# A landmark-attention, FFN and routed-experts kernel: where its zeros are stored, and the order in which its first batch is emitted

## The chip, the cores and the metric

The kernel runs on one core of one Trainium2 chip. The metric is the device time of one execution in microseconds (us); three executions of the kernel before took 683.63, 684.98 and 687.62 us, so its median is 684.98 us. The profile was taken in a further execution that took 681.71 us. The engines are named as the profile names them: PE (TensorE, the matmuls), PEld (its weight loads), DVE (VectorE), ACT (ScalarE), POOL (GpSimd) and SP (SyncE, which here issues nearly all DMAs, one after the other; SPq is its DMA queue).

## What is computed

The reference chains three parts. The shapes are 4 batches, 8 heads, 576 tokens, head size 64, so 2304 tokens of 512 numbers.

```
q_lm, k_lm = means of q, k over 32 groups of 18 tokens
A, B, C = softmax(q k_lm'), softmax(q_lm k_lm'), softmax(q_lm k)
Z = B' / (norm1(B) * norminf(B) + 1e-6);  six times: Z = 2 Z - Z B Z
x = A Z C v                                  # -> 2304 x 512
x = relu(x w_in)**2 w_out                    # w_in 512x2048, w_out 2048x512
logits = x w_gate                            # 8 experts
each token goes to its best expert e (at most 576 tokens in one):
out[token] = prob(e) * (relu(x w1[e]) w2[e]) # w1 512x1024, w2 1024x512
```

The FFN weights w_in and w_out arrive as 64-bit floats, and the chip has to make 32-bit ones of their two words.

## The kernel before, in words

**Precision.** The matmuls of FFN and experts take operands in a short float format. Each operand is split into a high and a low part (h and l at the end of a name: `gh`, `gl`, `ah`, `al`, the pairs of `w` and `mw`), and three products are summed. Making these parts costs DVE and ACT work beside each PE group.

**Conversion of the weights.** `Convert` does one of 32 units (16 of w_in, 16 of w_out) in steps, each of which is a letter in the tables below: `a` takes the words of the high half (L200 on DVE, or L202 on ACT), `b` those of the low half (L207, L209), `d` shifts and merges integers on DVE (L214, L215), `j` joins the two on DVE (L219), `s` rounds a w_out unit to its high part (L224 on DVE, or L226 on ACT), and `l` makes its low part (L229). The letters `h`, `c`, `t` and `p` are the same steps on the other engine. A joined pair of w_in units is stored in DRAM again (`w_in<-wi`, L1196) and read back later, one block of columns at a time (`wi<-w_in`, L514).

**Stages.** Per batch of 576 tokens: attention (jobs named K, Q, LK, LQ, BS, BE, BN, FR, C, CE, CM, N, T, CV, Z, SP, A, AE, AN), which ends in the matrix `mt` and in the pair `ah`, `al`; a projection, which folds `mt` into w_in (L531 matmuls, ACT copy L187, DVE L533) and gives `mw`; and the FFN. The FFN runs in two halves of 288 tokens over 16 chunks of 128 hidden numbers. A chunk is an "up" (six matmuls L544, then relu `r` L547 on ACT, square `gg` on ACT L550 or POOL L552, high part `gh` L555 on ACT, low part `gl` L558 on DVE) and, two chunks later, a "down" (twelve matmuls L564 into four accumulators `acc`). Batch 0 switches between its halves after 6, 12, 8, 4 and 2 chunks; at a switch DVE takes the accumulators over (`x<-acc,x`, L947), and the next down waits for that.

**After a half** is done an epilogue writes the tokens with their gate to the token table `x2d` in DRAM (`x2d<-xr`, L1012), and routing scatters their numbers to a table per expert (`tab`, POOL, L881). The rows of `x2d` that belong to batch 3 and the whole output are filled with zeros on the way (`x2d<-z`, `out_dram<-z`). The experts then run over gathered tokens and scatter their results.

**Order.** Per engine, instructions run in the order in which the program emits them, as a scheduler arranges it. `FIRST` is the order of the attention jobs and conversion steps of batch 0 ahead of the FFN. `PLAN` has one entry for each place between the groups of the FFN at which `fill()` may emit something else: E, M, A and X take the next job of the epilogue, the projection, the attention and the experts, and the letters take a conversion step. `ORDER` is the order of the attention jobs of the other batches. SP's queue, DVE and ACT work strictly through their rows, so that an instruction that waits holds up those behind it.

**The zeros.** `prefill()` runs behind the first finished half of batch 0. It makes a tile `z` of zeros on chip and issues the three small stores (L582 to L585) and the zeros of the late `x2d` rows: 96 x 24 runs of 128 numbers, 1152 KB (L588), and a small rest (L589). `CLEAR` names three halves, (1, 0), (1, 1) and (2, 0), and behind each of them `clear()` emits two of the six output stores of 768 KB (L597). Their only input is `z`, and the scheduler put all six next to those of `prefill()`.

Of the kernel before, what the change touches and what calls it, by code (L numbers as in the profile page):

```python
# [40 lines left out]
RB0 = 3.2  # L41
RB = 2.6

ORDER = "K0 K1 K2 K3 LK Q0 Q1 Q2 Q3 A00 LQ A01 BS AE0 C00 BE C01 BN AN0 C10 CM0 C11 FR CE0 CM1 N0 T00 CE1 N1 T01 SP0 N2 CV0 N3 A10 T10 N4 A11 T11 AE1 N5 CV1 AN1 Z SP1".split()
PLAN = (
    ".MdlAsddja .ptbt . .aapbl . .Ap . .dtbsdaljtdAl .A . .daAbdpaljtbjAdb .ptjj .dp . .j .a . .bd .tbttaphAap  "
    ".jbAbtMpaAA .b .dj .adjt . . . . . .apA .dp . .btAjdAAsappbdMjta .b . . . .jdl . .b . .jMjptlA . . . .ad . .l  "
    ".b . .b .jbAdjAAja . .adaM .sAd . . . .jAjlb .l .Attp .j .aAA . .ta .t .apba .Ad .j .Ad . .bAsApbd . .adb .b  "
    ".Mb .bjp . .Mlt . . .ldld .jt .bj . . . .Abb .tasAbAtA .j .lA .dMhtdAjA .dtA .AMdlb .pa . . .jjp . . . . . .At  "
# [3 lines left out]
).split()  # L53
FIRST = (
    "b K0 CO Q0 K1 K2 K3 Q1 Q2 Q3 LK LQ BS a BE BN FR C00 C01 j N0 CM0 d CE0 l a N1 N2 C10 b C11 a N3 j CM1 N4 h  "
    "T00 CE1 d T01 a d CV0 T10 b d T11 A00 j CV1 N5 Z p a b p A01 j d AE0 b AN0 j t j t b t d j SP0 a l "
).split()
P = 96
F32 = mybir.dt.float32
F32R = mybir.dt.float32r  # L60
# [14 lines left out]
def tile_landmark_attention__ffn__routed_experts(ctx, tc, q, k, v, w_in, w_out, w_gate, e_w1, e_w2, out, cap):  # L75
    nc = tc.nc
    B, _, H, _ = q.shape
    _, _, S, D = v.shape
    NT, DM = out.shape
# [5 lines left out]
    R = S // P  # L85
# [9 lines left out]
    K2 = F2 // 128  # L95
# [14 lines left out]
    x2d = tc.dram_tile([NT + 1, DM + 1], F32, name="x2d")  # L110
# [384 lines left out]
    def attention(b):  # L495
        names = attn_stages(b)
        return [job(names, n) for n in ORDER]

# [3 lines left out]
    def job(names, n):  # L502
        c = COST.get(n, COST.get(n[:2], COST[n[0]]))
        return (free if n[:2] == "SP" else always, names[n], c)
# [66 lines left out]
            tc.declare_no_dep(op.ins, o.ins.name, reason="each scatter writes the rows of other tokens")  # L571
        scatters[key].append(op)

    zero = []

    def prefill():
        def f():
            z = xp.tile([128, 128], F32, name="z")
            n = xp.tile([128, E * TE // 128], I32, name="n")
            nc.vector.memset(z, 0.0)  # L580
            nc.vector.memset(n, NT)
            nc.sync.dma_start(out=tab.rearrange("(p c) o -> p (c o)", p=128), in_=n)  # L582

            nc.sync.dma_start(out=x2d[NT:NT + 1, 0:DM], in_=z[0:4, :])
            nc.sync.dma_start(out=x2d[NT:NT + 1, DM:DM + 1], in_=z[0:1, 0:1])  # L585
            late = x2d[NT - S:NT, :].rearrange("(p r) x -> p (r x)", r=R)
            n = R * DM // 128
            nc.sync.dma_start(out=late[:, 0:n * 128].rearrange("p (c x) -> p c x", x=128), in_=z[:P, :].unsqueeze(1).to_broadcast([P, n, 128]))  # L588
            nc.sync.dma_start(out=late[:, n * 128:], in_=z[:P, 0:R])  # L589
            zero.append(z)  # L590
        return [f]

    def clear(i, of):
        def f():
            rows = out.rearrange("(p r) (c x) -> p (r c) x", p=128, x=128)
            n = rows.shape[1] // of
            nc.sync.dma_start(out=rows[:, i * n:(i + 1) * n, :], in_=zero[0].unsqueeze(1).to_broadcast([128, n, 128]))  # L597
        return f

    CLEAR = [(1, 0), (1, 1), (2, 0)]  # L600
# [353 lines left out]
    def epilogue(b, hf, acc):  # L954
# [51 lines left out]
        def store():  # L1006
            xr = s["xr"]
            sm = xp.tile([P, RP], F32, tag="sm", name="sm", bufs=2)
            nc.vector.tensor_reduce(out=sm, in_=s["ex"], axis=AX.X, op=ALU.add)
            nc.vector.tensor_scalar_add(sm, sm, 1e-9)  # L1010
            nc.vector.reciprocal(out=xr[:, :, DM], in_=sm)
            nc.sync.dma_start(out=x2d[b * S:(b + 1) * S, :].rearrange("(p r a) c -> p a r c", p=P, a=2)[:, hf], in_=xr)  # L1012

        st = [rows(1), rows(2), store]
        head = {0: [logits, token_logits, gates, rows(0)], 1: [logits, rows(0), token_logits, gates], 2: [logits, rows(0), rows(1), token_logits, gates]}[EO]
# [2 lines left out]
        if hf == (LAST0 if b == 0 else 1):  # L1018
# [12 lines left out]
            n = len(st)  # L1031
# [12 lines left out]

    planq = deque(x[1:] for x in PLAN)
    tick, clock, gstep, slow = [None], [0], [0], [0]
# [37 lines left out]
    def ffn(seq, before, after):  # L1084

        pend, acc = deque(), None
        for t in range(len(seq) + 2):
# [215 lines left out]
    for i, n in enumerate(RUNS):  # L1303
        hf = i % 2
# [42 lines left out]
```

## Time and profile before

| | us |
|---|---|
| median of three runs | 684.98 |
| the profiled execution | 681.71 |
| its span in the trace | 679.7 |
| PE busy | 616.6 (91%) |
| DVE busy | 342.6 (50%) |
| ACT busy | 302.1 (44%) |
| POOL busy | 119.1 (18%) |

Busy time is a sum over the span, and a stage can be bound by an engine whose sum is small. A view by windows tells where each engine is full. Each row of a list of instructions has its start, its duration, the engine, the line and the tiles, and in brackets the idle time of that engine just before it with what ended it. The granted clock of PE is given as a share of its full speed (1.00 is 2.4 GHz, 0.50 is 1.2 GHz).

### The profile page before, as it was taken

What the parts mean: (1) busy time and instruction counts of PE and PEld (TensorE: products, weight loads), DVE (VectorE), ACT (ScalarE), POOL (GpSimd) and SP (SyncE); (2) the same over time, 40 slices, a digit from 0 to 9 for tenths busy, and PEclk for the clock granted to TensorE, in tenths of its full rate; (3) what the DMA queues carried; (4) which work ended last, traced back from release to release, by engine and by line L of the source; (5) the groups of instructions that cost most, each with busy time, mean ns of one, the idle gap of its engine ahead of it and who ended that gap; (6) DMA issues with size and microseconds to landing.
All of it is one profiled execution on the core that took longest, in us unless ns stands there. A gap on an engine that the chain in (4) does not pass through costs nothing. (4 is left out here: it accounts for less than half of the span.)

```text
span 679.7 us, 13567 instructions
## 1 busy us (share of the span) xinstructions
PE 616.6 (91%) x5322; PEld 523.6 (77%) x5322; DVE 342.6 (50%) x915; ACT 302.1 (44%) x710; POOL 119.1 (18%) x152
## 2 busy tenths in 40 slices
PE   3158779999798999999999999999999999999993
PEld 1035658988686878888889888889998889789792
DVE  8998998634642364532363533335543515416310
ACT  4863756554434453444354444245522524415420
POOL 0000000000012021222431212442315013104101
PEclk9999869999899999999999999999999999999997
DMA  9996442499136122331400022333307417306400
GB/s 317 378 401 182 163 124 70 158 212 278 63 103 100 56 70 71 107 123 65 80 20 21 17 94 94 66 104 99 93 9 230 154 34 256 100 16 208 159 10 35
DMA packets 44021, 83.91 MB, mean 123 GB/s; under 512 B 7494, under 2 KB 22090, under 8 KB 43178
## 3 DMA queue, kind: packets, MB, share of 16 engines
q1 hardware_dynamic: 40762, 75.18, 37.3%
q0 software_dynamic: 3184, 7.75, 3.4%
q8 instruction: 45, 0.74, 0.5%
q14 instruction: 30, 0.25, 0.1%
HBM read 64.52 MB, written 18.39 MB: 122 GB/s over the span
## 5 line engine op out<-in xcount | busy, mean ns | idle before, releaser
L564 PE MATMUL acc<-gh,w 128*128 128x288 f32 x1024 | 234.8, 303 | 7.0 <-DVE x L947 3.4
L564 PEld LDWEIGHTS acc<-gh,w 128*128 128x128 f32 x1024 | 173.3, 191 | 19.0 <-issue 7.5
L564 PE MATMUL acc<-gl,w 128*128 128x288 f32 x512 | 153.1, 303 | 0.0
L544 PE MATMUL hp<-ah,mw 128*128 128x288 f32 x512 | 131.7, 311 | 2.4 <-ACT mw L187 1.4
L558 DVE TENSOR_TENSOR gl<-gg,gh 128x288 fp32r<-128x288 f32 x128 | 60.5, 474 | 97.9 <-POOL gg L552 59.5
L544 PEld LDWEIGHTS hp<-ah,mw 128*128 128x128 f32 x512 | 91.7, 194 | 16.7 <-issue 10.6
L564 PEld LDWEIGHTS acc<-gl,w 128*128 128x128 f32 x512 | 97.2, 190 | 8.0 <-issue 4.7
L547 ACT ACTIVATE r<-hp 128x288 f32<-128x288 f32 x128 | 51.8, 409 | 99.5 <-PE hp L544 98.4
L552 POOL TENSOR_TENSOR gg<-r 128x288 f32<-128x288 f32 x80 | 54.9, 688 | 196.9 <-ACT r L547 184.2
L544 PE MATMUL hp<-al,mw 128*128 128x288 f32 x256 | 78.1, 306 | 0.0
L685 PE MATMUL acc<-w,ehh 128*128 128x512 f32 (+1 forms) x240 | 76.0, 397 | 0.0
L881 POOL DMA_INDIRECT tab<-toks,slot x24 | 22.6, 941 | 222.1 <-ACT gh L555 198.9
L555 ACT ACTIVATE gh<-r 128x288 fp32r<-128x288 f32 x128 | 56.1, 440 | 9.8 <-PE acc L564 5.5
L677 DVE SCALAR_TENSOR_TENSOR ehl<-hp,ehh 128x320 fp32r<-128x320 f32 (+1 forms) x48 | 21.9, 456 | 65.4 <-ACT ehh L676 65.4
L544 PEld LDWEIGHTS hp<-al,mw 128*128 128x128 f32 x256 | 50.0, 195 | 1.7 <-issue 1.5
L685 PEld LDWEIGHTS acc<-w,ehh 128*128 128x128 f32 (+1 forms) x240 | 41.6, 177 | 11.6
L685 PE MATMUL acc<-w,ehl 128*128 128x512 f32 (+1 forms) x120 | 47.3, 394 | 0.0
L533 DVE TENSOR_TENSOR mw<-ps,mw 128x256 fp32r<-128x256 f32 x64 | 25.4, 419 | 40.9 <-ACT mw L187 40.8
L187 ACT ACTIVATE mw<-ps 128x256 fp32r<-128x256 f32 x64 | 22.5, 383 | 49.4 <-PE ps L531 49.3
L676 ACT ACTIVATE ehh<-hp 128x320 fp32r<-128x320 f32 (+1 forms) x48 | 19.7, 411 | 43.9 <-PE hp L672 41.6
L531 PE MATMUL ps<-wi,mt 64*32 64x256 f32 x512 | 32.1, 407 | 5.1 <-DMA wi<-w_in 1.8
L689 ACT ACTIVATE y<-acc,gt 128x512 f32<-128x512 f32 (+1 forms) x15 | 10.3, 686 | 56.2 <-PE acc L685 41.3
(253 smaller groups left out, 947.9 us busy)
## 6 DMA issues: line engine op xcount, KB each, us to landing
raw<-in_moe_w_dram SPq DMA_DIRECT2D x32, 512.0 KB, 4.7
wi<-w_in SPq DMA_DIRECT2D x24, 512.0 KB, 3.4
w<-in_moe_w_in_dram SPq DMA_DIRECT2D x16, 512.0 KB, 8.8
w<-in_moe_w_out_dram SPq DMA_DIRECT2D x16, 512.0 KB, 11.9
x2d<-xr SPq DMA_DIRECT2D x8, 577.1 KB, 4.6
out_dram<-z SPq DMA_DIRECT2D x6, 768.0 KB, 10.7
w_in<-wi SPq DMA_DIRECT2D x8, 512.0 KB, 6.0
kT<-in_k_dram SPq DMA_DIRECT2D x3, 1152.0 KB, 9.0
```

Source lines behind the costliest of these rows:

```text
L187: nc.scalar.activation(out=o, in_=i, func=AF.Copy)
L531: nc.tensor.matmul(out=ps[s, :FC], lhsT=mt[rows, c, :], rhs=wi[rows, c, :], start=True, stop=True)
L533: nc.vector.tensor_tensor(out=ml[:, g, :], in0=ps[:, :FC], in1=f32(mh[:, g, :]), op=ALU.subtract)
L544: nc.tensor.matmul(out=hp[:, :HB], lhsT=st[:, g, fs], rhs=mv[:, g, :], start=n == 0, stop=n == 5)
L547: nc.scalar.activation(out=r, in_=hp[:, :HB], func=AF.Relu)
L552: nc.gpsimd.tensor_tensor(out=gg, in0=r, in1=r, op=ALU.mult)
L555: nc.scalar.activation(out=gh, in_=r, func=AF.Square)
L558: nc.vector.tensor_tensor(out=gl, in0=gg, in1=f32(gh), op=ALU.subtract)
L564: nc.tensor.matmul(out=acc[d][:, :HB], lhsT=w2[fc][:, st, ds], rhs=mv, start=first and i == 0, stop=last and i == 2)
L677: nc.vector.scalar_tensor_tensor(out=hl[:, f, :n], in0=hp[:, :n], scalar=0.0, in1=f32(hh[:, f, :n]), op0=ALU.max, op1=ALU.subtract)
L685: nc.tensor.matmul(out=acc[:n, :], lhsT=h[:, f, off:off + n], rhs=w2[f][:, w, :], start=f == 0 and a == 0, stop=f == K2 - 1 and a == 2)
L881: return lambda: scattered("tab", nc.gpsimd.indirect_dma_start(out=tab[:, :], out_offset=bass.IndirectOffsetOnAxis(ap=sl[:, r:r + 1], axis=0),
```

## The change

Two things. The first: the two zero stores of the late `x2d` rows leave `prefill()` and go to the first `clear()`, and everything in `clear()` is emitted behind the last stored token rows (`tc.issue_after(stored[-1])`); the store L1012 puts itself on that list. The second: new tables. In `ORDER` the job CM0 stands ahead of AN0. `FIRST` and `PLAN` are rewritten; the tables hold the same jobs, and over both of them two roundings of w_out units go from DVE to ACT and one `a` step from ACT to DVE.

```diff
-ORDER = "K0 K1 K2 K3 LK Q0 Q1 Q2 Q3 A00 LQ A01 BS AE0 C00 BE C01 BN AN0 C10 CM0 C11 FR ...
+ORDER = "K0 K1 K2 K3 LK Q0 Q1 Q2 Q3 A00 LQ A01 BS AE0 C00 BE C01 BN CM0 AN0 C10 C11 FR ...
-PLAN = (
-    ".MdlAsddja .ptbt . .aapbl . .Ap . .dtbsdaljtdAl .A . .daAbdpaljtbjAdb .ptjj .dp . .j .a . .bd .tbttaphAap  "
...
+PLAN = '.lMalAsdtd .bjs .p .aabl .A .AAapp . .taljAtdbA .jdAd .s .tdAbalpjtbAdb .pdtjj .djp . . .a .d .dat .bspha ...
-    "b K0 CO Q0 K1 K2 K3 Q1 Q2 Q3 LK LQ BS a BE BN FR C00 C01 j N0 CM0 d CE0 l a N1 N2 C10 b C11 a N3 j CM1 N4 h  "
-    "T00 CE1 d T01 a d CV0 T10 b d T11 A00 j CV1 N5 Z p a b p A01 j d AE0 b AN0 j t j t b t d j SP0 a l "
+FIRST = 'Q0 K0 CO b K2 K3 K1 Q3 Q2 LK Q1 LQ BS BE BN FR C00 j b C01 N0 d CM0 N1 l CE0 a N2 C10 b C11 N3 N4 a CM1 h a d j T00 CE1 T01 d CV0 T10 T11 A00 j CV1 b N5 p d Z a b A01 b d j p AE0 b j t d t t j a AN0 SP0'.split()
 P = 96
...
-    zero = []
+    zero, stored = [], []
 
     def prefill():
         def f():
...
             nc.sync.dma_start(out=x2d[NT:NT + 1, 0:DM], in_=z[0:4, :])
             nc.sync.dma_start(out=x2d[NT:NT + 1, DM:DM + 1], in_=z[0:1, 0:1])
-            late = x2d[NT - S:NT, :].rearrange("(p r) x -> p (r x)", r=R)
-            n = R * DM // 128
-            nc.sync.dma_start(out=late[:, 0:n * 128].rearrange("p (c x) -> p c x", x=128), in_=z[:P, :].unsqueeze(1).to_broadcast([P, n, 128]))
-            nc.sync.dma_start(out=late[:, n * 128:], in_=z[:P, 0:R])
             zero.append(z)
         return [f]
 
     def clear(i, of):
+
         def f():
-            rows = out.rearrange("(p r) (c x) -> p (r c) x", p=128, x=128)
-            n = rows.shape[1] // of
-            nc.sync.dma_start(out=rows[:, i * n:(i + 1) * n, :], in_=zero[0].unsqueeze(1).to_broadcast([128, n, 128]))
+            z = zero[0]
+            with tc.issue_after(stored[-1]):
+                if i == 0:
+                    late = x2d[NT - S:NT, :].rearrange("(p r) x -> p (r x)", r=R)
+                    n = R * DM // 128
+                    nc.sync.dma_start(out=late[:, 0:n * 128].rearrange("p (c x) -> p c x", x=128), in_=z[:P, :].unsqueeze(1).to_broadcast([P, n, 128]))
+                    nc.sync.dma_start(out=late[:, n * 128:], in_=z[:P, 0:R])
+                rows = out.rearrange("(p r) (c x) -> p (r c) x", p=128, x=128)
+                n = rows.shape[1] // of
+                nc.sync.dma_start(out=rows[:, i * n:(i + 1) * n, :], in_=z.unsqueeze(1).to_broadcast([128, n, 128]))
         return f
...
-            nc.sync.dma_start(out=x2d[b * S:(b + 1) * S, :].rearrange("(p r a) c -> p a r c", p=P, a=2)[:, hf], in_=xr)
+            stored.append(nc.sync.dma_start(out=x2d[b * S:(b + 1) * S, :].rearrange("(p r a) c -> p a r c", p=P, a=2)[:, hf], in_=xr).ins)
```

What the tables do to the engines shows in the order of their instructions. Line numbers of the kernel after are smaller by 11 ahead of the zeros and by 7 behind them; a number behind a name tells tiles of one name apart.

**SP, from the first small zeros on.** `vt`, `qT` and `ld` are loads of batch 2, the last row of the first piece is a load of a block of w_in. Before:

```order
L582 DMA tab<-n 128x40
L585 DMA x2d<-z 1x1
L588 DMA x2d<-z 96x24x128
L589 DMA x2d<-z 96x6
L597 DMA out_dram<-z 128x12x128 x6
L514 DMA wi<-w_in_69 128x1024
L277 DMA vt<-in_v_dram 96x4x384
L238 DMA qT<-in_q_dram 128x2304
L273 DMA ld<-in_v_dram 96x2x384 x2
```

After, from the store of the first half of batch 1 on (here `vt`, `qT` and `ld` are those of batch 3):

```order
L227 DMA kT<-in_k_dram 128x2304
L1005 DMA x2d<-xr 288x1x513
L586 DMA x2d<-z 96x24x128
L587 DMA x2d<-z 96x6
L590 DMA out_dram<-z 128x12x128 x2
L266 DMA vt<-in_v_dram 96x4x384
L227 DMA qT<-in_q_dram 128x2304
L262 DMA ld<-in_v_dram 96x2x384 x2
L503 DMA wi<-w_in_69 128x1024 x6
L1005 DMA x2d<-xr 288x1x513
L590 DMA out_dram<-z 128x12x128 x2
```

The large zeros went from ahead of the loads of batch 2 to behind the stores of batch 1 and 2, and the first group of them now stands ahead of the loads of batch 3; the last two output stores follow the next store of token rows.

**DVE, at the switch of halves in batch 0** at which the four sums `x<-acc,x` free the accumulators. `partq` is made from `qT` of batch 2. Before:

```order
L251 TENSOR_REDUCE partq<-qT 128x64 x4
L462 TENSOR_TENSOR T<-T,asm 128x576
L558 TENSOR_TENSOR gl<-gg,gh 128x288
L947 TENSOR_TENSOR x_1630<-acc_2030,x_1630 128x288
L947 TENSOR_TENSOR x_1630<-acc_2031,x_1630 128x288
L469 STREAM_TRANSPOSE at<-T 128x576
L947 TENSOR_TENSOR x_1630<-acc_2032,x_1630 128x288
```

After:

```order
L240 TENSOR_REDUCE partq<-qT 128x64 x4
L450 RECIPROCAL asm<-asm 128x18
L940 TENSOR_TENSOR x_1606<-acc_2025,x_1606 128x288
L940 TENSOR_TENSOR x_1606<-acc_2026,x_1606 128x288
L547 TENSOR_TENSOR gl<-gg,gh 128x288
L940 TENSOR_TENSOR x_1606<-acc_2027,x_1606 128x288
L940 TENSOR_TENSOR x_1606<-acc_2028,x_1606 128x288
L451 TENSOR_TENSOR T<-T,asm 128x576
```

The sums moved ahead of the attention's division of `T` and of the transpose into `at`; `partq` stays ahead of them.

**ACT, between the first chunks of the FFN.** `w_953` and `w_981` before, `w_956` and `w_982` after, are w_out units that have just been loaded. Before:

```order
L187 ACTIVATE mw<-ps 128x256 x2
L202 ACTIVATE w_953<-w_953 128x512
L209 ACTIVATE w_953<-w_953 128x512
L547 ACTIVATE r<-hp 128x288
L202 ACTIVATE w_981<-w_981 128x512
L550 ACTIVATE gg<-r 128x288
L555 ACTIVATE gh<-r 128x288
L209 ACTIVATE w_981<-w_981 128x512
```

After:

```order
L539 ACTIVATE gg<-r 128x288
L544 ACTIVATE gh<-r 128x288
L176 ACTIVATE mw<-ps 128x256
L198 ACTIVATE w_956<-w_956 128x512
L439 ACTIVATE T<-T 128x576
L191 ACTIVATE w_982<-w_982 128x512
L198 ACTIVATE w_982<-w_982 128x512
```

Relu and square of the third chunk stood behind the first conversion of a new unit; now the chunks' steps stand ahead of it (four chunks are through by then), and the other half of that step, L200, went to DVE.

## Rows read from the trace of the kernel before

**Rows 1.** Windows: busy us (instructions) of each engine, granted clock, DMA share, GB/s.

```profile
51.00:68.00 17.00, 13.69 (x105) 9.05 (x104) 15.00 (x31) 6.75 (x17) 0.00 (x0) 1.00 0.62 183
68.00:85.00 17.00, 13.37 (x102) 10.64 (x102) 15.84 (x34) 12.07 (x30) 0.00 (x0) 0.90 0.48 162
85.00:102.00 17.00, 12.99 (x90) 9.09 (x91) 16.52 (x38) 9.33 (x23) 0.00 (x0) 0.70 0.42 124
102.00:119.00 17.00, 17.00 (x143) 15.12 (x142) 15.22 (x38) 10.40 (x28) 0.00 (x0) 1.00 0.23 71
```

**Rows 2.** Timeline of PE: idle time ahead of matmuls of the ramp.

```profile
53.98 0.61 PE L544 MATMUL hp<-ah,mw 128*128 128x288 f32 x1 [1.36 <-ACT mw L187]
...
70.89 1.33 PE L564 MATMUL acc<-gh,w 128*128 128x288 f32 x4 [2.06 <-ACT gh L555]
...
87.09 0.69 PE L436 MATMUL ps<-qT,lmk 64*32 64x288 f32 x8 [2.33 <-DVE mw L533]
```

**Rows 3.** Timeline of ACT: waits for loaded units, and what stood behind one.

```profile
68.08 0.72 ACT L202 ACTIVATE w<-w 128x512 f32<-128x512 f32 x1 [7.05 <-DMA w<-in_moe_w_out_dram]
...
88.38 0.70 ACT L202 ACTIVATE w<-w 128x512 f32<-128x512 f32 x1 [3.44 <-DMA w<-in_moe_w_in_dram]
...
89.50 0.67 ACT L187 ACTIVATE ah<-at 128x576 fp32r<-128x576 f32 x1
```

**Rows 4.** Timeline of DVE: steps of the conversion.

```profile
57.62 0.65 DVE L219 CUSTOM_DVE_ANT_0 ct<-w,ct 128x1024 uint16<-128x1024 uint16 x1
58.31 0.43 DVE L224 CAST w<-ct 128x512 fp32r<-128x512 f32 x1
58.77 0.69 DVE L229 TENSOR_TENSOR w<-ct,w 128x512 fp32r<-128x512 f32 x1
59.49 0.43 DVE L214 TENSOR_SCALAR ct<-w 128x512 int32<-128x512 int32 x1
...
60.23 0.68 DVE L215 SCALAR_TENSOR_TENSOR ct<-w,ct 128x512 int32<-128x512 int32 x1
```

**Rows 5.** Timelines of SP's queue and DVE: the queries of batch 1, asked for and used.

```profile
65.38 0.33 SPq L238 DMA_DIRECT2D qT<-in_q_dram  x1
...
75.09 2.74 DVE L251 TENSOR_REDUCE partq<-qT 128x64 f32<-128x576 f32 x4
```

**Rows 6.** Timeline of SP's queue: the output zeros, and the queries of batch 2.

```profile
136.12 18.68 SPq L597 DMA_DIRECT2D out_dram<-z  x6
...
159.75 0.35 SPq L238 DMA_DIRECT2D qT<-in_q_dram  x1
```

**Rows 7.** Timelines of DVE and PE at the switch of halves in batch 0.

```profile
169.53 2.73 DVE L251 TENSOR_REDUCE partq<-qT 128x64 f32<-128x576 f32 x4 [5.02 <-DMA qT<-in_q_dram]
...
173.22 0.81 DVE L947 TENSOR_TENSOR x<-acc,x 128x288 f32<-128x288 f32 x2
...
173.72 0.61 PE L564 MATMUL acc<-gh,w 128*128 128x288 f32 x1 [3.42 <-DVE x L947]
```

**Rows 8.** Windows (columns as in rows 1) during the zeros, and around that switch.

```profile
140.00:145.00 5.00, 5.00 (x65) 4.54 (x50) 2.00 (x5) 2.69 (x8) 0.00 (x0) 1.00 1.22 137
...
150.00:155.00 5.00, 5.00 (x55) 4.28 (x55) 1.33 (x4) 2.02 (x6) 0.00 (x0) 1.00 1.11 326
...
170.00:175.00 5.00, 1.58 (x21) 1.28 (x6) 5.00 (x11) 0.91 (x3) 0.00 (x0) 0.83 0.31 106
175.00:180.00 5.00, 5.00 (x37) 4.26 (x35) 3.76 (x10) 0.77 (x2) 0.00 (x0) 0.83 0.00 0
```

**Rows 9.** The page's DMA issues: KB each, median us from issue to landing.

```profile
out_dram<-z SPq DMA_DIRECT2D x6, 768.0 KB, 10.7
...
x2d<-z SPq DMA_DIRECT2D x1, 1152.0 KB, 14.5
```

**Rows 10.** Timelines of SP's queue and DVE in batch 1, where the zeros go.

```profile
258.95 0.56 SPq L1012 DMA_DIRECT2D x2d<-xr  x1
...
276.42 0.34 SPq L238 DMA_DIRECT2D qT<-in_q_dram  x1
...
282.27 2.75 DVE L251 TENSOR_REDUCE partq<-qT 128x64 f32<-128x576 f32 x4 [0.66 <-DMA qT<-in_q_dram]
```

**Rows 11.** Timeline of PE: a wait behind the scatters of batch 0.

```profile
215.21 0.62 PE L531 MATMUL ps<-wi,mt 64*32 64x256 f32 x4 [1.78 <-DMA wi<-w_in]
```

More of the change, by code (lines that the diff above doesn't have):

```diff
@@ L42 @@
 RB = 2.6
-ORDER = "K0 K1 K2 K3 LK Q0 Q1 Q2 Q3 A00 LQ A01 BS AE0 C00 BE C01 BN AN0 C10 CM0 C11 FR CE0 CM1 N0 T00 CE1 N1 T01 SP0 N2 CV0 N3 A10 T10 N4 A11 T11 AE1 N5 CV1 AN1 Z SP1".split()
-PLAN = (
-    ".MdlAsddja .ptbt . .aapbl . .Ap . .dtbsdaljtdAl .A . .daAbdpaljtbjAdb .ptjj .dp . .j .a . .bd .tbttaphAap  "
-    ".jbAbtMpaAA .b .dj .adjt . . . . . .apA .dp . .btAjdAAsappbdMjta .b . . . .jdl . .b . .jMjptlA . . . .ad . .l  "
-    ".b . .b .jbAdjAAja . .adaM .sAd . . . .jAjlb .l .Attp .j .aAA . .ta .t .apba .Ad .j .Ad . .bAsApbd . .adb .b  "
-    ".Mb .bjp . .Mlt . . .ldld .jt .bj . . . .Abb .tasAbAtA .j .lA .dMhtdAjA .dtA .AMdlb .pa . . .jjp . . . . . .At  "
[3 rows of a table removed]
-).split()
-FIRST = (
-    "b K0 CO Q0 K1 K2 K3 Q1 Q2 Q3 LK LQ BS a BE BN FR C00 C01 j N0 CM0 d CE0 l a N1 N2 C10 b C11 a N3 j CM1 N4 h  "
-    "T00 CE1 d T01 a d CV0 T10 b d T11 A00 j CV1 N5 Z p a b p A01 j d AE0 b AN0 j t j t b t d j SP0 a l "
-).split()
+ORDER = "K0 K1 K2 K3 LK Q0 Q1 Q2 Q3 A00 LQ A01 BS AE0 C00 BE C01 BN CM0 AN0 C10 C11 FR CE0 CM1 N0 T00 CE1 N1 T01 SP0 N2 CV0 N3 A10 T10 N4 A11 T11 AE1 N5 CV1 AN1 Z SP1".split()
+PLAN = '.lMalAsdtd .bjs .p .aabl .A .AAapp . .taljAtdbA .jdAd .s .tdAbalpjtbAdb .pdtjj .djp . . .a .d .dat .bspha .bMbpA .jAabd .d .ajt . .t . .jl . .AapA .d .bb .bjdtaatppbddMj .blt .A . . .jj .b . . .jptj . .A .p .d . .laj .bA .d .b .jAa .Aba .tAadaM . .p .A . .jAjb .td .A .Aj .AalA .ap .tp .tA .bMh .l .dbaj .Ad . .bsb . .dd .Apb .Mjb .bjp .Ma .ls . .A .d .tj .Mj .l . .l .bt .tsAAcAA .jtt .cl .dhhAj .A .AMdl .pA . .t .pt .db . . . . .Aj . .ddAA . .p . . . . . . .A .A .A .d . . .Mt . .tbA .A . .A . .h .Ad . .a . .Aa .A .A . . . . . . .M . .A . .j .l . . . . . . . . . .E .EElEA .E .E . .a . . . . . .EEE .EE . .E . . . .EEE .ME .E . . . . . . .EEs . . .lEMEE .bM .EEEA . . . . . . . . . . . . .j .sA'.split()
+FIRST = 'Q0 K0 CO b K2 K3 K1 Q3 Q2 LK Q1 LQ BS BE BN FR C00 j b C01 N0 d CM0 N1 l CE0 a N2 C10 b C11 N3 N4 a CM1 h a d j T00 CE1 T01 d CV0 T10 T11 A00 j CV1 b N5 p d Z a b A01 b d j p AE0 b j t d t t j a AN0 SP0'.split()
 P = 96
```

3 rows, old and new, of the table PLAN are left out of this document.

## The prediction

> **What bounds the kernel now.** I read the windows first, since 91% busy of PE hides where it is not. PE is full from about 100 us on, but in the three windows from 51 to 102 us it is busy 13.69 + 13.37 + 12.99 = 40.05 of 51 us [rows 1]: 10.95 us are idle, and in two of them the granted clock is under 1.00. There DVE is busy 47.36 of 51 us. So the ramp, where the weights are still being converted, is bound by DVE, with 3.64 us in which DVE too waits; at 102 to 119 us PE has taken over. Next I read the timeline of PE for what ends its gaps [rows 2]: copies of ACT (`mw`, `gh`) and DVE's `mw`. The waits of ACT tell why ACT is late though it is half idle: it stood 7.05 us at a freshly asked w_out unit and 3.44 us at a w_in unit [rows 3], with relu, `gh` and `ah` queued behind. Last, the only wide gap after the ramp is 3.42 us at 173.72 [rows 7]: PE waits for the sums that free its accumulators, these stand on DVE behind `partq`, and `partq` had waited 5.02 us for `qT`. The load was asked for at 159.75 and in use at 169.53, 9.78 us; that of the next batch took 276.42 to 282.27, 5.85 us [rows 6, 10]. What lies between is 1152 KB + 6 x 768 KB of zeros, whose last issue ends at 154.80 [rows 6, 9].
>
> **The change part by part.** The sum is made against the profiled execution, 681.71 us, which is 3.27 us (0.48%) under the median of the runs shown; I add these 3.27 us at the end.
>
> *1. Zeros out of the way of `qT` of batch 2.* The load has its 5.85 us again instead of 9.78, so `partq` may start 3.93 us earlier, and the DVE wait of 5.02 us falls to about 1.1. In the new order two of the sums stand ahead of what was in front of them (division and `gl`). PE's gap of 3.42 us should so go down to 0 to 1.5 us; I take 0.5, for the load is still asked for only after the matmuls that read the tile's last content. The clock: 0.83 in both five-us windows from 170 to 180 [rows 8], which between the levels 1.0 and 0.5 is a third of 10 us, 3.4 us, at the lower one. Part of that was idle; the matmuls after 173.72 lost about 1 us to it. Gain 2.9 + 1.0 = **3.9 us**, with bounds 2.5 and 4.8 (nothing of the gap left, and 1.4 us of clock).
>
> *2. Zeros in their new places.* The first group is 1152 + 2 x 768 KB = 2.75 MB, behind the store at 258.95. By the rates at which the zeros ran before, 137 GB/s for the `x2d` rows and 326 GB/s later [rows 8], that is 1.18 MB / 0.137 + 1.57 MB / 0.326 = 8.6 + 4.8 = 13.4 us: done at about 273 us. `qT` of batch 3 is asked for at 276.42 [rows 10], 3 us later, and DVE waited only 0.66 us for it, with PE at work. `vt`, between them on the queue, is half its size and can start some us late without holding up DVE, which doesn't read it. I take **0**, with bounds 0 and +2 us (zeros a few us longer than that, seen first by `partq`). The two later groups (1.57 MB each, 4.8 us) have no load behind them that is needed soon.
>
> By the Trainium skill ("DMA: Bandwidth & Descriptors", section "Queues, rings and completion order") each DMA engine takes the descriptors of one issuing engine's ring in their order, so that a load waits for zeros queued ahead of it and not just for a share of the bandwidth; that speaks against this place too, and is the mechanism of the third rival. The 9.78 against 5.85 us of the `qT` loads agrees with it; which of the two it was no row can tell.
>
> *3. The ramp.* The conversion stays: three instructions in all change engines, two roundings at 0.43 us from DVE to ACT and one step back, under 0.5 us. What counts is what stands on DVE ahead of an instruction for which PE waits. I counted this along the two orders: ahead of the seventh `gl`, three roundings, one join, one low part, and one each of the two merging steps less, and one `a` step (a copy like the rounding) more. With their durations [rows 4] that is 3 x 0.43 + 0.65 + 0.69 + 0.43 + 0.68 - 0.43 = 3.3 us; instructions follow each other up to 0.1 us closer than that, which leaves 2.8. Ahead of the 13th and the 17th it is about 3.5, so the lead is kept up to where PE becomes full. To this comes part of the 3.64 us in which DVE itself waited: joins that waited for a buffer PE still read now have `mw` and `at` ahead of or between them, and the wait for the w_out unit on ACT, with the 2.06 us gap of PE behind it [rows 2], goes, since four chunks of relu and `gh` stand ahead of it. The same holds for `ah`, which ran at 89.50 behind the unit that ACT waited 3.44 us for [rows 3] and now stands ahead of it. I take 2.3 us of the 3.64, and 3.2 for the lead: **5.5 us**, with bounds 2 (half the lead is lost to waits that come up elsewhere, and no DVE wait is saved) and 7.5 (all DVE waits, 3.9 of lead). A lead of the first "up" alone (`vblk` and the first `mw` stand ahead of 2 to 3 us of attention work that was ahead of them) is in this and not beside it.
>
> *4. Behind the scatters.* PE waited 1.78 us at 215.21 for a block of w_in [rows 11]; more of these loads now go ahead of the second store of tokens, and the projection is spread out in pieces. I take **1 us**, bounds 0 and 2.5 (with smaller gaps nearby). From about 240 us on PE, DVE, ACT and POOL have the same rows in the same order, so the tail is worth 0.
>
> Sum: -3.9 + 0 - 5.5 - 1 = -10.4: 681.71 - 10.4 = 671.3, and with the 3.27 us, **674.6 us**. The ends together give -14.8 (670.2) and -2.5 (682.5).
>
> **The rivals.**
>
> *Only the zeros count.* The new tables give as much as they take: a lead on one chain is a lag on another, and DVE, which bounds the ramp, has the same work. For it: DVE busy 16.52 of 17 us at 85 to 102 leaves nothing to close up there. Against it: PE's gaps there belong to named instructions that the order moves forward. Then -3.9 - 0.5 = -4.4: 680.6 us.
>
> *A new wait in the ramp.* `partq` of batch 1 moved up on DVE (row 153 to row 141, 7.0 us less work ahead of it, counted as in part 3), while `qT` for it was asked for at 65.38 and `partq` ran at 75.09 without a wait [rows 5]. By its place it would now run at 68.1. If the load still goes out at 65.4 it lands at 71.2 to 75.2 (5.85 to 9.78 us), and DVE stands for 3.1 to 7.1 us with `gl` and `mw` behind it: the 5.5 us of part 3 are gone, and up to 2 more. It decides from an issue later than 62.2. Against it: in the new order `qT` stands ahead of the second store of w_in, behind which it was held, and the matmuls that free its tile stand ahead of the first down, so I expect the issue by 60. Result: -4.9 + 0 to +2: 680 to 682.
>
> *Slower: the zeros hold up batch 3.* If the three stores of the first group do not overlap, they take 14.5 + 2 x 10.7 = 35.9 us [rows 9] and end at 259.5 + 35.9 = 295.4; `qT` then lands at 301.3 instead of 282.27, `partq` stands on DVE for 19 us, and `gl` behind it stops PE for nearly as long, as at 173.72, where 3.93 us of lateness cost a gap of 3.42. With gains of 10.4 that is 681.71 - 10.4 + 19 + 1.5 of lower clock + 3.27 = 695 us. It decides from an end of the zeros at about 286 us, where what is lost equals what is won; slower by over 0.5% from about 290 on. Against it: six output zeros were issued within 18.68 us, and at 326 GB/s they did overlap.
>
> *The change doesn't do what it says.* The stores surely move, but if `qT` of batch 2 is late for another reason (its own issue at 159.75, behind the matmuls that read the old tile) the gap of 3.42 us stays: -6.5, 678.5 us.
>
> **How the numbers follow.** A difference under 0.5% (3.4 us) is about what a measurement of this kernel cannot tell from none, so faster means under 681.6. Forecast (670 to 678) 0.60; only the zeros 0.15 (seven tenths of it below 681.6); a new wait in the ramp 0.11, half below; change without effect at `qT` 0.05; slower by held-up loads 0.06; 0.03 for more than the sum's lower end. Faster: 0.60 + 0.10 + 0.04 + 0.05 + 0.02 = 0.81, which I cut to 0.78 for what I have not seen; same 0.15; slower 0.07. The range reaches from the lower end, 670, to 682, so that it holds the first two rivals but no more; it leaves out the slower one and the worst of the ramp.
>
> **What would show it.** In the profile after: `partq` of batch 2 without a wait of over 1.5 us, and no PE gap over 1.5 us ahead of the down at the switch, clock 1.00 there; DMA share near 1 at 260 to 273 us, and `qT` of batch 3 in under 7 us; PE full some 5 us sooner, by 97 us; no ACT wait of several us with a relu behind it; `qT` of batch 1 asked for by 60 us. What would make it wrong: a DVE wait at `partq` in batch 1 or batch 3, or PE gaps in the ramp that add up to 10.95 us again.

## The result

The kernel after takes 667.02 us (median of 4 runs, 664.99 to 671.36) beside 684.31 us of the kernel before (median of 4): a ratio of 0.9727, 95% interval 0.9676 to 0.9778 (the ratio is estimated from the single executions; the two medians alone divide to 0.9747). By the medians that is 17.3 us less, where 10.4 were forecast, and it lies 3 us under the lower end of the range. The direction was right, the size was not. The profiled executions differ by 681.71 - 664.99 = 16.72 us, so the two traces can be set against each other.

First the windows of the kernel after, those of [rows 1] (busy us and instruction count of PE, PEld, DVE, ACT, POOL, then the granted clock, DMA share and GB/s):

```profile
51.00:68.00 17.00, 15.50 (x118) 10.54 (x110) 16.70 (x34) 10.27 (x27) 0.00 (x0) 1.00 0.83 250
68.00:85.00 17.00, 14.05 (x111) 10.09 (x112) 17.00 (x40) 9.86 (x22) 0.00 (x0) 0.84 0.40 124
85.00:102.00 17.00, 17.00 (x116) 14.20 (x116) 16.09 (x40) 11.86 (x29) 0.00 (x0) 0.75 0.34 93
102.00:119.00 17.00, 17.00 (x149) 14.96 (x147) 16.33 (x41) 10.37 (x29) 0.00 (x0) 1.00 0.50 164
```

PE is busy for 46.55 us of the first three windows instead of 40.05, and DVE for 49.79 instead of 47.36: it hardly waits any more. Next come the gaps of PE over 1 us from 55 to 450 us, all there are (timeline of PE, idle time in brackets):

```profile
68.32 0.40 PE L553 MATMUL acc<-gl,w 128*128 128x288 f32 x1 [1.82 <-DVE gl L547]
...
81.76 0.70 PE L249 MATMUL ps<-partq,jmat 128*128 128x256 f32 x2 [1.97 <-DVE mw L522]
...
201.24 0.67 PE L520 MATMUL ps<-wi,mt 64*32 64x256 f32 x16 [1.37 <-DMA wi<-w_in]
...
271.05 0.43 PE L410 MATMUL ps<-vblk,cv 128*64 128x128 f32 x2 [1.69 <-DVE cv L403]
```

None of them is at the switch of halves in batch 0, and one is new, at 271.

Gaps and clock alone do not add up to 16.7 us, so I set up an account that takes in what a busy PE loses as well: for each matmul the time from its start to the next start, less the median of that time for the same form of matmul in the trace of before, summed up by stage. The stages end at points of the program: the first "up", the 7th down, 9 us ahead of and 4.3 us behind the 31st down (the switch), 1.5 us behind the 47th, the 63rd. A fixed amount of it is in each kernel; the differences count. Below, "lost" means this quantity.

| PE time above the median spacing, us | before | after | difference | forecast |
|---|---|---|---|---|
| up to the first "up" | 38.7 | 36.7 | -2.0 | in the ramp |
| ramp, to the 7th down | 25.7 | 19.3 | -6.4 | -5.5 |
| to the switch | 10.2 | 10.8 | +0.6 | 0 |
| the switch | 5.9 | 2.1 | -3.8 | -3.9 |
| behind it, to the 47th down | 18.3 | 12.8 | -5.5 | -1 |
| to the 63rd down (first zeros) | 10.4 | 11.2 | +0.8 | 0 |

The sum is -16.3 us; from the 63rd down on all downs come 16.4 us earlier than before, up to the last. The term that fails is the forecast's fourth part, behind the switch, 4.5 us more than forecast, and with less weight the ramp, 2.3 us more (8.4 less the 0.6 given back, against 5.5).

What happens behind the switch shows in the blocks of the projection. A projection of one block of w_in consists of two halves of eight matmuls (one on rows 0 to 63 of the array, one on rows 64 to 127). Timeline of PE in the kernel before, each block with the row behind it:

```profile
204.57 0.64 PE L531 MATMUL ps<-wi,mt 64*32 64x256 f32 x8
205.13 0.40 PE L544 MATMUL hp<-ah,mw 128*128 128x288 f32 x1
...
206.25 0.64 PE L531 MATMUL ps<-wi,mt 64*32 64x256 f32 x8
206.82 0.40 PE L544 MATMUL hp<-ah,mw 128*128 128x288 f32 x1
```

And in the kernel after, in the same stage:

```profile
193.43 0.66 PE L520 MATMUL ps<-wi,mt 64*32 64x256 f32 x16
194.02 0.80 PE L553 MATMUL acc<-gh,w 128*128 128x288 f32 x4
...
197.94 0.66 PE L520 MATMUL ps<-wi,mt 64*32 64x256 f32 x16
198.53 0.54 PE L533 MATMUL hp<-ah,mw 128*128 128x288 f32 x2
```

A block of 8 holds PE for 0.56 to 0.57 us, one of 16 for 0.59: the halves run side by side if nothing stands between them. Even a block of 4 takes nearly as long, 0.55 us from its start to that of the next row, as this one of the kernel before:

```profile
217.02 0.62 PE L531 MATMUL ps<-wi,mt 64*32 64x256 f32 x4
217.57 0.40 PE L544 MATMUL hp<-ah,mw 128*128 128x288 f32 x1
```

So it is the number of blocks that costs, hardly the number of matmuls in them. With what entry and exit cost (0.09 and 0.11 us over the usual spacing, from all 42 blocks of these two sizes in the kernel before) a block of 8 costs 0.76 us and one of 16 costs 0.79, so each cut pair costs some 0.74 us more. The same 112 matmuls stand between the switch and the 47th down in 14 blocks before and in 9 after: 5 x 0.74 = 3.7 us, and the gaps there fell from 3.15 to 1.83 us, 1.3 more. Together that is 5.0 of the 5.5. The granted clock was 1.00 in this stage in both traces, so it has no part in the difference.

### The profile page after: what moved, and what is told of

Its sections match the earlier page's. It is cut to its first block, busy times and chain, and to the rows that moved or that the text cites. A ratio compares the mean times of both kernels' runs of the same rounds, so it can differ in the third digit from the quotient of the medians.

```text
span 663.2 us, 13569 instructions
## 1 busy us (share of the span) xinstructions
PE 611.8 (92%) x5322; PEld 521.4 (79%) x5322; DVE 341.1 (51%) x914; ACT 302.5 (46%) x711; POOL 118.4 (18%) x152
## 5 line engine op out<-in xcount | busy, mean ns | idle before, releaser
L533 PE MATMUL hp<-ah,mw 128*128 128x288 f32 x512 | 130.0, 310 | 0.0
L670 DVE SCALAR_TENSOR_TENSOR ehl<-hp,ehh 128x320 fp32r<-128x320 f32 (+1 forms) x48 | 21.9, 456 | 65.4 <-ACT ehh L669 65.4
L522 DVE TENSOR_TENSOR mw<-ps,mw 128x256 fp32r<-128x256 f32 x64 | 25.2, 416 | 35.9 <-ACT mw L176 35.8
L683 POOL DMA_INDIRECT out_dram<-y,it x15 | 14.8, 985 | 114.4 <-ACT y L682 109.5
```

What stands on the lines that cost most here:

```text
L522: nc.vector.tensor_tensor(out=ml[:, g, :], in0=ps[:, :FC], in1=f32(mh[:, g, :]), op=ALU.subtract)
L533: nc.tensor.matmul(out=hp[:, :HB], lhsT=st[:, g, fs], rhs=mv[:, g, :], start=n == 0, stop=n == 5)
L670: nc.vector.scalar_tensor_tensor(out=hl[:, f, :n], in0=hp[:, :n], scalar=0.0, in1=f32(hh[:, f, :n]), op0=ALU.max, op1=ALU.subtract)
```

## The experiments

The kernel before ran beside each. Its medians there were 678.9 us (zeros alone; tables alone, first run; tables in two parts), 680.2 us (the kernel before again, cut pairs, the kernel after again and its zeros later) and 681.5 us (FIRST alone, PLAN alone; tables alone, second run). Ratios are against these. The expectations count from 684.3 us, so it is their differences that can be compared. In the diffs of the tables `_BEFORE` and `_AFTER` stand for the tables of the two kernels, and `[:150]` for the first 150 entries.

**The old tables, the zeros in their new places.**

```diff
-ORDER, PLAN, FIRST = ORDER_AFTER, PLAN_AFTER, FIRST_AFTER
+ORDER, PLAN, FIRST = ORDER_BEFORE, PLAN_BEFORE, FIRST_BEFORE
```

> The old tables with the zeros in their new places. By the account of PE's time by stages, the zeros are worth two terms: the wait at the switch of halves in batch 0, with its slow clock, goes (-4.0 us), and the queries of batch 3 land late behind the first group of zeros (+1.7 us). So about -2.3 us against the kernel before, 682 us, with no PE gap over 1 us at the switch and a DVE wait of 4 to 5 us at `partq` of batch 3. Rival, the tables did it all: the switch keeps its gap of 3.4 us and the time is 684 to 686 us.

677.87 us, ratio 0.9981 (0.9947 to 1.0016): 1.0 us less, where 2.3 were expected, and not to be told from no change. In its trace the two mechanisms are there. DVE at `partq` of batch 2, then of batch 3 (timeline):

```profile
164.30 2.75 DVE L251 TENSOR_REDUCE partq<-qT 128x64 f32<-128x576 f32 x4 [0.28 <-DMA qT<-in_q_dram]
...
281.20 2.74 DVE L251 TENSOR_REDUCE partq<-qT 128x64 f32<-128x576 f32 x4 [3.39 <-DMA qT<-in_q_dram]
```

The first wait, 5.02 us in [rows 7], is nearly gone; the second is 3.39 us instead of 0.66 us [rows 10]. The stage of the switch lost 2.5 us of PE time instead of 5.9. Behind it there are 13 blocks and 19.2 us lost, about as before (14 and 18.3). So the zeros alone move a wait from one batch to the next one, and what it costs there is less (PE gap 0.29 us).

**The kernel before a second time.**

> The kernel before once more, for a second trace of it: the same stages as in the first, with 3 to 4 us of gap at the switch of halves in batch 0 and 13 or 14 blocks of the projection behind it; the ramp's gaps may differ by 1 to 3 us with the landing of the loaded weights.

One execution, 680.28 us. This trace brought down the largest term that I had read from the first. DVE at the switch:

```profile
165.81 2.74 DVE L251 TENSOR_REDUCE partq<-qT 128x64 f32<-128x576 f32 x4 [1.63 <-DMA qT<-in_q_dram]
...
169.51 0.81 DVE L947 TENSOR_TENSOR x<-acc,x 128x288 f32<-128x288 f32 x2
```

`qT` was asked for at the same point (159.43) and took 6.4 us instead of 9.78, since the zeros and the loads `wi` and `vt` queued behind them had come through some 1 to 3 us earlier; DVE waited 1.63 us, and PE did not wait at all: the switch lost 2.6 us. PE's wait was not a fixed cost of the kernel before but one that one of its two traces has. In exchange the stage behind it lost 21.9 us, with one gap of 1.95 us and a granted clock of 0.55 and 0.50 in the ten us from 210 on.

**The new tables, the zeros in their old place,** in two separate runs. Only the first part of the diff is printed.

```diff
             nc.sync.dma_start(out=x2d[NT:NT + 1, DM:DM + 1], in_=z[0:1, 0:1])
+            late = x2d[NT - S:NT, :].rearrange("(p r) x -> p (r x)", r=R)
+            n = R * DM // 128
+            nc.sync.dma_start(out=late[:, 0:n * 128].rearrange("p (c x) -> p c x", x=128), in_=z[:P, :].unsqueeze(1).to_broadcast([P, n, 128]))
+            nc.sync.dma_start(out=late[:, n * 128:], in_=z[:P, 0:R])
...
-            with tc.issue_after(stored[-1]):
...
```

> The new tables with the zeros where they were before. Stage account: ramp and what follows it -7.1 us, the stage behind the scatters -5.4 us, the switch unchanged because `qT` of batch 2 again waits behind the zeros, no delay in batch 3: -12.5 us, 672 us, and a DVE wait of 4 to 5 us at `partq` of batch 2. Rival, the sums ahead of the attention work on DVE would have removed the wait at the switch without the zeros: 665 to 667 us and no PE gap there.

> The new tables with the zeros in their old place, once more, to have it with more rounds. If the old place costs what its first trace showed (a DVE wait of 2.3 us at `partq` of batch 2, a PE gap of 1.4 us and 0.8 us of lower clock behind it), it is 2 to 4 us above the kernel after, 667 to 669 us. Rival, the old place costs nothing on average: 664 us.

669.26 us, ratio 0.9884 (0.9783 to 0.9985), and 668.98 us, ratio 0.9832 (0.9795 to 0.9868). The wait at the switch is there again with the new tables, though the sums now stand ahead of the attention work (first run):

```profile
162.62 2.73 DVE L240 TENSOR_REDUCE partq<-qT 128x64 f32<-128x576 f32 x4 [2.27 <-DMA qT<-in_q_dram]
165.45 0.75 DVE L936 TENSOR_TENSOR x<-acc,x 128x288 f32<-128x288 f32 x2
...
165.89 0.47 PE L553 MATMUL acc<-gh,w 128*128 128x288 f32 x1 [1.40 <-DVE x L936]
```

So the sums' order does not do it, and the rival of that falls. The stage lost 5.0 and 4.0 us (2.1 in the kernel after), so with the new tables the old place costs 2 to 3 us there. What it costs as a whole is not settled: the ratios lie 0.007 and 0.012 above that of the kernel after again (0.9764, below), 5 and 8 us, but all three intervals overlap. Nor do the parts add up: 1.3 us for the zeros alone and 8 to 11 us for the tables alone, by their ratios, stand against 16 to 19 us for both. Where the rest comes from no run here separates.

**The tables in two parts, cut at entry 150 of PLAN.** At that place both plans have emitted the same jobs and, by the letters of the tables, the same conversion steps but for one `a` and one `b`; it lies just ahead of the first epilogue. First the new head with the old tail, then the old head with the new tail, both with the zeros in their new places.

```diff
-ORDER, PLAN, FIRST = ORDER_AFTER, PLAN_AFTER, FIRST_AFTER
+ORDER, PLAN, FIRST = ORDER_AFTER, PLAN_AFTER[:150] + PLAN_BEFORE[150:], FIRST_AFTER
...
+ORDER, PLAN, FIRST = ORDER_BEFORE, PLAN_BEFORE[:150] + PLAN_AFTER[150:], FIRST_BEFORE
```

> New places of the zeros, FIRST, ORDER and the first 150 entries of PLAN new, the other 52 entries old. Stage account: -7.1 (ramp) -4.0 (switch) +1.7 (batch 3) = -9.4 us, 675 us, with the projection behind the switch cut in 13 or 14 blocks as before and 5 us more of PE time lost between the switch and 240 us than in the kernel after. Rival, the whole gain of the tables is the ramp's lead, carried on: 667 to 669 us.

> New places of the zeros, FIRST, ORDER and the first 150 entries of PLAN old, the other 52 entries new. Stage account: -4.0 (switch) +1.7 (batch 3) -5.4 (behind the scatters, fewer blocks of the projection and shorter waits) = -7.7 us, 676.6 us. Rival, the whole gain of the tables is the ramp's: 681 to 682 us, as with the zeros alone.

673.36 us, ratio 0.9903 (0.9869 to 0.9936), and 671.59 us, ratio 0.9888 (0.9794 to 0.9982): 5.5 and 7.3 us less than the kernel before, where 9.4 and 7.7 were expected. The new tail alone does much of it, against the rival by which all is the ramp's; and it does so from a ramp that lost as much as before (26.4 us). The stage behind the switch, in these and their neighbours:

| | blocks | PE time lost, us | gaps of PE, us | ratio |
|---|---|---|---|---|
| zeros only (old head, old tail) | 13 | 19.2 | 3.2 | 0.9981 |
| old head, new tail | 9 | 12.4 | 0.9 | 0.9888 |
| new head, old tail | 14 | 22.7 | 5.1 | 0.9903 |
| after again | 9 | 13.1 | 2.1 | 0.9764 |

From the first line to the second, four blocks fewer (3.0 us) and 2.3 us less of gaps are 5.3 of the 6.8 us; in the first the granted clock was besides at 0.66 in the five us behind its largest gap, a third of 5 us at full speed and two thirds at the lower level, which is another 1.7 us (timeline of PE, then windows, zeros only):

```profile
204.64 0.64 PE L531 MATMUL ps<-wi,mt 64*32 64x256 f32 x8 [2.72 <-DMA wi<-w_in]
...
205.00:210.00 5.00, 5.00 (x34) 4.62 (x30) 0.88 (x2) 1.04 (x3) 0.00 (x0) 0.66 0.40 97
```

The third line has one large gap (SP's queue, then PE):

```profile
189.30 0.57 SPq L1005 DMA_DIRECT2D x2d<-xr  x1
192.15 4.36 SPq L503 DMA_DIRECT2D wi<-w_in  x2
...
201.55 1.08 PE L520 MATMUL ps<-wi,mt 64*32 64x256 f32 x8 [5.09 <-DMA wi<-w_in]
```

A block of w_in asked for at 192.15, right behind the store of tokens and in the midst of the scatters to `tab`, landed at 201.41, 9.3 us later; the median of these loads is 3.2 us in this run. In the kernel after, SP had issued three of these loads ahead of that store and PE waited 1.37 us.

**FIRST alone and PLAN alone,** with the new ORDER and the new places of the zeros.

```diff
-ORDER, PLAN, FIRST = ORDER_AFTER, PLAN_AFTER, FIRST_AFTER
+ORDER, PLAN, FIRST = ORDER_AFTER, PLAN_BEFORE, FIRST_AFTER
...
+ORDER, PLAN, FIRST = ORDER_AFTER, PLAN_AFTER, FIRST_BEFORE
```

> The new FIRST and ORDER and the new places of the zeros, with the old PLAN. If the lead of the ramp comes from the first tables of the attention, PE's first up comes about 2 us earlier as in the kernel after, and no more than that is kept: -2 us in the head, the ramp's loss as before (25 us of PE time by the stage account), 13 or 14 blocks behind the switch: 675 to 677 us. Rival, FIRST carries the whole ramp: 670 us. By its order 21 pairs of halves are cut here instead of 12, which costs up to 7 us wherever PE is full, so it can also come out slower than that.

> The new PLAN and ORDER and the new places of the zeros, with the old FIRST. If PLAN carries what moved, the ramp loses about 20 us of PE time as in the kernel after, the first up comes at 54 us as before, and there are 9 or 10 blocks behind the switch: 667 us. Rival, the two tables only work together: 672 us or more.

677.07 us, ratio 0.9932 (0.9905 to 0.9959), and 665.95 us, ratio 0.9773 (0.9733 to 0.9812). Against the kernel before that is 4.4 and 15.5 us less; some 8 and 17 were expected. PLAN carries it: the second ratio is within the interval of the kernel after's. (Both runs have the new ORDER, which was not tried by itself; with FIRST and the zeros it is worth no more than the first of these ratios.) The windows of the second over the ramp (columns as above):

```profile
51.00:68.00 17.00, 15.93 (x86) 11.07 (x88) 16.51 (x34) 8.26 (x20) 0.00 (x0) 1.00 0.73 232
68.00:85.00 17.00, 13.57 (x110) 9.99 (x110) 16.47 (x38) 10.79 (x27) 0.00 (x0) 0.90 0.45 146
85.00:102.00 17.00, 16.52 (x147) 13.00 (x146) 16.77 (x41) 12.41 (x32) 0.00 (x0) 1.00 0.32 93
```

Its ramp lost 19.0 us, as that of the kernel after, though its first up came at 53.1, 1.2 us later. With FIRST alone it came at 51.7 and the ramp lost 21.4, but the stage that follows lost 17.3 instead of 10.2, with two blocks more and a granted clock of 0.53 from 85 to 102 us. The lead in time was handed back there, mostly at the lower clock.

**Cut pairs.** The kernel after, in which both halves of a projection in batches 1 to 3 write the same bank. The second half has then also to wait until ACT and DVE have read the first out of it, so the edit can add gaps besides the cut.

```diff
+            ps = pm.tile([128, 512], F32, tag="m", name="ps")
             for g in range(2):
                 rows = slice(64 * g, 64 * g + 64)
-                ps = pm.tile([128, 512], F32, tag="m", name="ps")
+                if b < 1 and g:
+                    ps = pm.tile([128, 512], F32, tag="m", name="ps")
```

> The kernel after, but in batches 1 to 3 both halves of a projection use the same accumulator bank, so that the second cannot run right behind the first. By the order this makes 12 more blocks of the projection, with the same matmuls, copies and tiles. In the traces a block of 8 matmuls takes PE 0.76 us and one of 16 takes 0.79 us, with what its entry and exit cost, so 12 more blocks cost 12 x 0.74 = +8.9 us. Rival, blocks are free because the matmuls are the same: 0 to +2 us.

683.46 us, ratio 1.0049 (1.0019 to 1.0078), 19.8 us above the kernel after beside it, where 8.9 were expected: the whole gain is gone and more. Behind the 63rd down, where PE is full, the price can be read by itself: 27 blocks instead of 19, and 35.8 us lost instead of 28.0. Of the difference 0.7 are gaps, which leaves 7.1 us for 8 blocks, 0.89 each, where 0.74 was expected; the rival by which blocks are free falls. The surplus lies in the stage behind the switch: 13 blocks instead of 9 and 22.4 us lost instead of 13.1. Four blocks account for 3 us of that; PE waited 4.96 us for a block of w_in here, as with the new head and old tail above, so its gaps are 3.2 us more than in the kernel after again, and the granted clock was 0.50 in the five us from 205 on, which is some 2 us. Whether the cut pairs bring the late load about is not separated there. The ramp's 2.4 us more are not explained by the edit, which leaves batch 0 as it was; two other runs with the ramp of the kernel after (the new head with the old tail, and the new tables with the zeros in their old place, first run) have the same 21 us, so the ramp runs in one of two ways.

**The kernel after again, and its zeros one store later.**

```diff
-    CLEAR = [(1, 0), (1, 1), (2, 0)]
+    CLEAR = {(1, 1): (0, 1, 2, 3), (2, 0): (4, 5)}
...
-            st += [clear(2 * CLEAR.index((b, hf)) + i, 2 * len(CLEAR)) for i in range(2)]
+            st += [clear(i, 6) for i in CLEAR[b, hf]]
```

> The kernel after once more, unchanged, beside the experiments of this chip: 664 to 668 us, and by stages of PE the same account as in its first trace: no gap at the switch, nine blocks of the projection behind it, and a DVE wait of 4 to 5 us at `partq` of batch 3 with a PE gap of 1 to 2 us behind it.

> The kernel after with the large zeros one store later: the late token rows and four output stores behind the second half of batch 1, two output stores behind the first half of batch 2. The queries of batch 3 then have no zeros ahead of them on SP's queue. If the zeros cost what the trace of after says, `qT` of batch 3 lands in under 7 us, the DVE wait and the PE gap behind it go, and the time is 1.7 us below after. Rival, the wait is from the load's own late issue: no change.

663.62 us, ratio 0.9764 (0.9725 to 0.9802), and 664.67 us, ratio 0.9778 (0.9741 to 0.9815): no gain, and my expectation of -1.7 us falls. In the first trace of the kernel after the zeros did cost (SP's queue, DVE, and the windows):

```profile
240.61 0.60 SPq L586 DMA_DIRECT2D x2d<-z  x1
...
246.69 6.01 SPq L590 DMA_DIRECT2D out_dram<-z  x2
252.80 5.60 SPq L266 DMA_DIRECT2D vt<-in_v_dram  x1
258.50 0.45 SPq L227 DMA_DIRECT2D qT<-in_q_dram  x1
...
268.07 2.73 DVE L240 TENSOR_REDUCE partq<-qT 128x64 f32<-128x576 f32 x4 [4.75 <-DMA qT<-in_q_dram]
```

```profile
245.00:250.00 5.00, 5.00 (x93) 4.66 (x94) 2.64 (x6) 2.27 (x7) 0.67 (x1) 1.00 1.21 133
250.00:255.00 5.00, 5.00 (x54) 4.11 (x53) 1.15 (x4) 1.97 (x6) 1.33 (x2) 1.00 1.23 131
255.00:260.00 5.00, 5.00 (x54) 4.11 (x53) 2.46 (x6) 1.69 (x5) 0.67 (x1) 1.00 1.02 236
260.00:265.00 5.00, 5.00 (x91) 4.20 (x90) 2.15 (x7) 2.20 (x6) 0.78 (x2) 1.00 1.03 340
```

The zeros landed at 261.44, 20.8 us after their first issue, and `qT`, asked for at 258.50, took 9.5 us; DVE stood for 4.75 us, and PE for 1.69 us (the gap at 271). The window from 260 on holds hardly any zeros any more: its 340 GB/s are `vt` and `qT`. In the second trace the same DVE row reads:

```profile
265.77 2.74 DVE L240 TENSOR_REDUCE partq<-qT 128x64 f32<-128x576 f32 x4 [2.30 <-DMA qT<-in_q_dram]
```

and PE has no gap there. With the zeros later `qT` still took 7.0 us, with none ahead of it, DVE waited 1.60 us, and the stage behind the switch came out a little worse (14.7 us lost). So the place behind batch 1's first half costs PE 1.7 us in one trace and nothing in the other, and the median of the later place is not better.

## Why the forecast was wrong, point by point

**Ramp: right mechanism, size 5.5, measured 7.8 to 8.4.** Head and ramp together lost 8.4 us less, 7.8 with the 0.6 us given back up to the switch. The signs that were named came: DVE busy 49.79 of 51 us, PE at the 7th down at 89.6 instead of 98.2 and without a gap from there to the switch, `qT` of batch 1 asked for at 58.07 instead of 65.38 [rows 5], no wait of ACT for a load above 0.5 us in 56 to 84 us, where one of 7.05 had stood [rows 3]. The seventh `gl` tells the two terms apart (timeline of DVE, before and after):

```profile
96.21 0.45 DVE L558 TENSOR_TENSOR gl<-gg,gh 128x288 fp32r<-128x288 f32 x1
...
89.76 0.44 DVE L547 TENSOR_TENSOR gl<-gg,gh 128x288 fp32r<-128x288 f32 x1
```

It comes 6.45 us earlier. Up to it DVE had stood idle for 7.50 us before and for 3.85 after, 3.65 less; the other 2.8 us are work that no longer stands ahead of it, as counted. So the lead was right, and the mis-sized term is the waits of DVE, 2.3 us taken and 3.65 measured (4.2 up to the 13th `gl`): part of them lie ahead of 51 us, outside the windows from which I took the 3.64. The upper bound, 7.5, was passed. PLAN carries it, not the head of FIRST, on which I had put a lead of the first up: that was worth 2 us there, and alone it was given back.

**The switch: the forecast -3.9 met -3.8 in the two traces, but it was no fixed gain.** That the two agree is in part luck. I took one execution's wait for the kernel's: the same kernel has the wait or not, as its second trace shows, and the interval of the zeros alone, from 0.9947, leaves at most 3.6 us for the whole change of place. The packet records of a trace (the pieces in which a DMA moves: 512 bytes each for the zeros, 9216 for `qT`) tell more. In the two traces of the kernel before the last packet of the zeros ends at 159.55 and 158.27, and `qT` is asked for at 159.75 and 159.43: what stood ahead of it by then were `wi` and `vt`, held back by the zeros, and some 1 to 2 us decide whether PE waits. The rival by which `qT` is late for another reason falls: with the zeros alone moved DVE's wait went from 5.02 to 0.28 us.

**The zeros' new place: 0, bounds 0 and +2, measured +0.8 and -0.9 in the two traces of the kernel after.** The sign that was named for it, `qT` of batch 3 in under 7 us, did not come: it took 9.5 and 7.5 us. The mis-sized piece is the time until the zeros are through, 13.4 us forecast, 20.8 measured in the first trace and 18.9 in the second. In the packets the zeros' own run is 17.7 and 15.7 us; the rest is the store of token rows, behind which they are queued and which I left out (the first zeros move 2.7 us after their issue), and the landing. The rate of the `x2d` rows was about right (131 to 133 GB/s in the first trace, where 137 were taken), that of the output zeros was not (236 GB/s in the window from 255 on, where 326 were taken); why it was lower is open. The slower rival had the right mechanism, zeros that hold up `qT` of batch 3, with a price of 1.7 us in one trace and not 19: its condition, three stores one after the other, did not hold, since they landed 2.1 and 2.3 us apart.

The Trainium skill ("DMA: Bandwidth & Descriptors", section "Queues, rings and completion order") says that a DMA engine takes the descriptors of one ring in their order. The packets of this case agree with it: in the first trace of the kernel after `vt` is asked for at 252.80 and its first packet moves at 259.05, `qT` at 258.50 and 261.13, just behind the last of the zeros (260.96). With nothing ahead of them the first packet of these loads moves 1.0 us after the request, as in the run with the zeros later. With a plain share of the bandwidth `vt` would not have stood for 6.3 us.

**Behind the scatters: -1 forecast, -5.5 measured; this is the step that failed.** I costed it by the gap of 1.78 us alone, and read the new order as one that spreads the projection out in pieces. It does that in the ramp (9 blocks instead of 6, where PE waits anyway); behind the switch it joins them, 9 instead of 14, worth 3.7 us, and 1.3 us of gaps went besides. The term that was left at nothing is the price of a cut pair. The rows were there to see: the halves stand as one row of 16 or as two of 8 in the order and in the timeline, and a busy PE hides the difference, since both count as full. PE's busy time as a whole fell by 4.8 us, from 616.6 to 611.8, with the same 5322 matmuls. The size depends on the execution too: between the second traces of the two kernels the same stage differs by 8.8 us, of which part is the lower clock behind a gap.

The Trainium skill ("TensorEngine Tiling (Array Packing)", section "Tiling Modes", under "Key Properties") states both halves of this: tiles of the array work in parallel, and a change of the tiling mode drains the engine. The rows agree (0.59 us for 16 matmuls on two sets of rows, 0.57 for 8 on one, and some 0.2 us at the two changes). Read against [rows 11], whose block of 4 is a cut one, it would have pointed to the missing term.

**The other rivals.** Only the zeros: wrong, it gave 680.6 and the tables alone have a ratio of 0.983 to 0.988. A new wait at `partq` of batch 1: it did not come, DVE ran it at 64.51 without a wait. The range's lower end, 670, added up bounds of which the fourth, 2.5, was far too tight because it was drawn from gaps alone. In the chances half of 0.11 was entered as 0.04, a slip that changes no conclusion.

## What to carry to other kernels

Where an engine counts as full, compare start to start, not idle times: the same matmuls cost 3.7 us less when small-tile groups stood next to each other, and no gap showed it. A wait on a transfer that is 2 us from being hidden is a property of an execution, so a term built on it wants a second trace. And a load queued behind bulk stores starts when they are through, so their duration has to be known: here 2.75 MB of zeros took 15.7 to 17.7 us, with the `x2d` rows at 131 to 137 GB/s, where the output zeros had reached 326. What a better place for them is worth stayed within the noise here (ratio 0.9981 with the old tables, and no gain from putting them later still).

## What the hardware showed that was not expected

Sixteen matmuls of 64 x 32 tiles on two sets of 64 rows took 0.59 us and eight on one set 0.57 us, so the second set is nearly free if it follows at once; cut off by a single full-size matmul it costs 0.74 to 0.89 us. And a lead can be lost to the clock: with the new FIRST and the old PLAN PE was busy all of the 17 us from 85 on, at a granted clock of 0.53, which between the levels of 1.2 and 2.4 GHz is almost wholly the lower (windows):

```profile
68.00:85.00 17.00, 12.84 (x105) 8.94 (x108) 17.00 (x38) 10.33 (x23) 0.00 (x0) 0.97 0.39 129
85.00:102.00 17.00, 17.00 (x93) 13.05 (x94) 14.72 (x36) 8.66 (x21) 0.00 (x0) 0.53 0.36 107
```

It counts 93 matmuls there, the kernel with the new PLAN and the old FIRST 147 at a clock of 1.00. The latter's clock had been lower for a while too (0.90 from 68 to 85 us). Ahead of its fall PE had waited 3.8 us in four gaps (76 to 84 us) in the one and 2.8 us in two (77 to 80 us) in the other; why the clock stayed down for so much longer in the one is not settled here.
